# Reordered evacuations and value stages in a one-core kernel of block-sorted attention and four experts

## The chip, the cores and the metric

The program runs on one core of a Trainium2 chip. The core has a matrix engine (TensorE, PE in the profile, with its weight loads as PEld), a vector engine (VectorE, DVE), a scalar engine (ScalarE, ACT), GpSimd (POOL) and SyncE (SP). Each engine works through its own instructions in order. Transfers are issued by SP, by ACT or by POOL and are moved by sixteen DMA engines that all queues share. Matrix products are written to PSUM, a small memory of eight banks, and one of DVE or ACT has to read them out ("evacuate" them) before a bank is used again. The metric is the device time of one execution in microseconds (us).

## The reference

Attention comes first. Its inputs q, k and v have 4 batches, 8 heads, 768 positions and 64 values a head; the positions form 8 blocks of 96. A matrix P of 8 x 8 per batch and head is made almost doubly stochastic by five rounds, and then mixes the blocks of k and v:

```python
for _ in range(5):
    P = np.exp(P - np.max(P, axis=-1, keepdims=True))
    P = P / (np.sum(P, axis=-1, keepdims=True) + 1e-09)
    P = P / (np.sum(P, axis=-2, keepdims=True) + 1e-09)
k_sorted = np.einsum('bhij,bhjcd->bhicd', P, k_b)    # the same for v
attn = softmax(scale * q_b @ k_sorted_b.T)           # within a block of 96
attn_out = attn @ v_sorted_b
```

The result is laid out as x with 3072 tokens of 512 values, and goes through four experts, weighted by the normalized domain probabilities p:

```python
out = 0
for e in range(4):
    out += p[:, e:e+1] * (np.maximum(x @ w1[e], 0) @ w2[e])   # w1: 512 x 1024, w2: 1024 x 512
```

## The kernel before

All matrices are held as 16-bit floats. The tokens are cut into twelve chunks of 256: three chunks (c = 0 to 2) for each of four batches (b = 0 to 3). The first layer of an expert on a chunk is `chunk_first` (L770): two groups of sixteen matmuls of 256 columns (L780), each into a PSUM tile `ps_h`. A matmul reads `xT`, the attention's result with the values along the partitions, in four slices `kc`; slice kc holds the head pair kc and is written by one DMA transpose. DVE evacuates a group by a relu times the expert's weight `pb` (L786) into `Hb`.

The second layer, and in the last stages the first one too, are done in a form of the Strassen-Winograd product: seven products of half-size blocks in place of eight, with sums of the blocks before and after. For the second layer the sums of activations are four DVE operations per expert, `h_sums(e, 1)` to `h_sums(e, 4)` (L750, L752, L754, L756), and for batch 0 the results are added into tiles in `room` (L872 to L896).

The order of the work is written by hand: the instructions are issued to the engines in the order of the program. Attention of the next batch is cut into stages (`st_v`, `st_q`, `st_k`, `st_s`, `st_a`, `st_x`, and loads `st_lv`, `st_lk`, `st_n`), and `PLANS` (L614) says after which step of which chunk each of them is issued: `(2, 7, st_v, 2, 0)` is issued in chunk 2 at slot 7, for batch 2 and head pair 0. Slots 0 to 5 follow the six groups of the first layer of a batch-0 chunk, slots 6 to 12 its second layer's products.

- `st_v(b, pr)` (L357) mixes the blocks of v for two heads: two PE matmuls of 384 columns into a PSUM tile of the pool `psA`, and one ACT copy into the tile `vo` in `arena` (L367). The second one of a group of four heads also issues six SP copies from `vo` to `vs` (L375).
- `st_a` (L438) multiplies the exponentials by `vs` (L449), and DVE normalizes the result into `xsl` (L430, L431). It uses `psA` too. The pool has two tiles, used in turn.
- `st_x` (L457) issues the DMA transpose of `xsl` into a slice of `xT` on SP (L465). `st_q` (L380) issues the transpose of q into `q_ring` on SP (L383), which `st_s` (L409, L414) reads. `load_p` (L211, L213) loads `pb` for a chunk on SP, after the first layer of the chunk before.
- SP works in the order of the program, so each of these transfers waits for the ones issued before it, and for a free one of eight completion semaphores.

The last stages begin at chunk 5 (`G0`), and then take the chunks 6 to 11 two at a time. `last_first` (L1160) runs the first layer as `seven(g, n)` (L1080): for each half expert n, seven products p1 to p7 of four matmuls (L1104) into the banks Z, X and Q. ACT copies Z to X after p1 (L1124), p2 adds to Z, and DVE finishes Z into `Hb` (`finish`, L1110); p6, p7 and p4 add to X, with ACT copies of X between them (L1131, L1139), and DVE finishes X. There are two X and two Z banks, used in turn. p1 to p7 of n and of n-1 are interleaved in the loop at L1182. `last_second` (L1199) is the second layer of 256 of these tokens, with its own sums of activations (L1222).

At the start POOL issues the loads of q, k, v, of expert 0's `w1` (two transfers, L134) and `w2` (one, L139), builds masks between them (L174 to L198), and PE runs matmuls on a constant tile `dummy` to keep warm (`warm`, L252; `keep_warm`, L474).

Of the kernel before, what the change touches and what calls it, by code (L numbers as in the profile page):

```python
# [17 lines left out]
def kernel(  # L18
# [11 lines left out]
    nc = tc.nc  # L30
# [104 lines left out]
                w1sb[e][:, ds(i * n, n)], moe_w1[e].rearrange("(kc p) f -> p kc f", p=P)[:, ds(i * n, n)]  # L135
            )

    def load_w2(e):
        nc.gpsimd.dma_start(w2sb[e][:], moe_w2[e].rearrange("(fc p) d -> p fc d", p=P))  # L139

    def load_half_queries(hf):
        for qd in range(2):
# [1 line left out]
                q0[ds(64 * qd, 64), hf].rearrange("p h r d -> p h (r d)"), half_queries(qd, hf)  # L144
            )

    dummy = Hflat[:, ds(2 * NFC * 2 * P, P)]
    nc.vector.memset(dummy, 0.5)


    NT = N // P
# [1 line left out]
    def p_part(at, n):  # L153
# [12 lines left out]
    load_natural(0, "v", 0)  # L166
    load_natural(0, "k", 1)
    load_natural(0, "v", 1)
    load_w1(0, 2)

    eye16 = const.tile([P, CP], F16, name="eye16")
    maskk = const.tile([P, P], F16, name="maskk")
# [5 lines left out]
        maskk.rearrange("p (i c) -> p i c", c=CP),  # L178
        eye16.rearrange("p (o c) -> p o c", o=1).broadcast_to([P, NB, CP]),
    )  # L180

    perm = const.tile([BLK, BLK], F16, name="perm")
    nc.gpsimd.tensor_copy(
# [90 lines left out]
    scol = const.tile([GH, NB, 1], F32, name="scol")  # L274
    sn16 = const.tile([GH, NB, NB, CP], F16, name="sn16")
    warm(84)
    p_steps = spread_weights()
    nc.gpsimd.tensor_copy(ident6, ident[0:R, 0:R])
    for it in range(5):
        nc.scalar.activation(sn[:], sn[:], AF.Exp, bias=0.0, scale=1.0)  # L280
        if it == 4:
            for qd in range(2):
                h_q(qd, 0, nc.scalar.copy)
            warm(30)
        nc.vector.tensor_reduce(srow[:], sn[:], AX.X, ALU.add)
# [195 lines left out]
    def mix_half(nm, qd, hf, pool, warm_up=0):  # L481

        ps = pool([P, 1024], F32, f"ps_m{nm}_{qd}_{hf}")
        keep_warm(ps[:, 0:P], warm_up)
        tails[(nm, qd, hf)] = ps[:, 2 * R * 64:1024].bitcast(F16).rearrange("p (n x) -> p n x", n=2)
        ps = ps[:, 0:2 * R * 64].rearrange("p (s r x) -> p s r x", s=2, r=R)
        for sg in range(2):
            for r in range(R):
                for hh in range(2):
                    h = 4 * qd + 2 * sg + hh  # L490
                    nc.tensor.matmul(
                        ps[ds(D * hh, D), sg, r, :],
                        head(0, nm, h)[:, r, :],
                        PI0[hf][:, h, :, :].rearrange("p i c -> p (i c)"),
                        start=True, stop=True,
                    )
        return ps
# [111 lines left out]
    def st_bk(b, qd):  # L609
# [10 lines left out]
            (1, 8, st_s, 1, 1), (1, 8, st_x, 1, 0), (1, 9, st_k, 1, 2), (1, 9, st_q, 1, 3), (1, 9, st_lv, 2, 1),  # L620
            (1, 11, st_a, 1, 1), (1, 12, st_lk, 2, 0),
            (2, 0, st_s, 1, 2), (2, 0, st_x, 1, 1), (2, 0, st_n, 2, 0), (2, 0, st_n, 2, 1), (2, 1, st_k, 1, 3),
            (2, 1, st_n, 2, 2), (2, 1, st_n, 2, 3), (2, 2, st_lk, 2, 1), (2, 3, st_a, 1, 2),
            (2, 4, st_x, 1, 2), (2, 4, st_q, 2, 0), (2, 5, st_s, 1, 3),
            (2, 5, st_q, 2, 1), (2, 6, st_a, 1, 3), (2, 7, st_v, 2, 0), (2, 8, st_x, 1, 3), (2, 8, st_v, 2, 1),
            (2, 9, st_k, 2, 0), (2, 9, st_lv, 3, 0), (2, 9, st_n, 3, 0), (2, 11, st_s, 2, 0), (2, 12, st_q, 2, 2),
        ],
        1: [
# [168 lines left out]
    def chunk(b, c, slot, done=()):  # L797
# [68 lines left out]
        if c:  # L866
            both = ob.rearrange("p (h d) -> p h d", h=2)
            times(bankA, blk(0, 0), "b11", es)
            slot()
            times(bankB, blk(1, 0), "b21", es)  # L870
            slot()
            tt(oa1, bankA, oa1, ALU.add)  # L872
            tt(oa1, bankB, oa1, ALU.add)
            h_sums(E - 1, 2)
            times(bankC, blk(1, 1), "n4", es[:1], True, False)
            times(bankQ, sm(0), "t1", es)
            tt(ob2, bankQ, ob2, ALU.add)
            slot()
            for e in es:
                h_sums(e, 3)  # L880
            for e in es:
                h_sums(e, 4)
            times(bankA, sm(1), "t2", es, False)
            tt(oa2, bankA, oa2, ALU.add)
            slot()
            next(sums0)
            times(bankC, blk(1, 1), "n4", es[1:], False)
            tt(ob1, bankC, ob1, ALU.add)
            slot()
            times(bankA, sm(2), "t3", es, False)  # L890
            tt(both, bankA.rearrange("p (o d) -> p o d", o=1).broadcast_to([P, 2, DH]), both, ALU.add)
            slot()
            store(1, ob)
            next(sums0)
            times(bankQ, sm(3), "b22", es, False)
            tt(oa2, bankQ, oa2, ALU.add)  # L896
            slot()
            store(0, oa)
            return
# [180 lines left out]
    def seven(g, n):  # L1080

        lead = g == G0
        if lead:
            e, f0, cols = n, 0, P
            pb = pbs[divmod(g, R // 2)]
            home = lambda i, j: Hb[:, e, ds(i * KH, KH), ds(j * P, P)]
            weight = lambda j: pb[:, ds(e, 1), ds(j * P, P)]
            n -= 1
            Q = last["Q"][(0, 0, 1, 3)[e]][:]
        else:  # L1090
            e, f0, cols = n // 2, n % 2 * 2, 2 * P
            home = lambda i, j: (last["H"][e] if j else Hb[:, e])[:, ds(i * KH + f0, 2), :]
            weight = lambda j: pbs[g](j, e)
            Q = last["Q"][n % 4][:]
        m = 512 // cols
        a, t = As[e], Bs[g]
        X, Z = [last[nm][n % len(last[nm])][:] for nm in ("X", "Z")]
        u2, u3, t22, t12 = [last[nm][n % len(last[nm])] for nm in ("u2", "u3", "t22", "t12")]
        tt = nc.vector.tensor_tensor

        def product(dst, lhs, rhs, first=False):
            for f in range(m):
                for k in range(2):
                    nc.tensor.matmul(  # L1104
                        dst[:, ds(f * cols, cols)], a[lhs][:, k, ds((f0 + f) * P, P)], t[rhs][:, k, :],
                        start=(first and f == 0 and k == 0), stop=(f == m - 1 and k == 1), skip_group_check=True,
                    )

        def finish(i, j, src):
            nc.vector.scalar_tensor_tensor(  # L1110
                out=home(i, j), in0=src.rearrange("p (f x) -> p f x", f=m), scalar=0.0,
                op0=ALU.max, in1=weight(j).broadcast_to([P, m, cols]), op1=ALU.mult,
            )

        def finish2(i, j, src):
            nc.scalar.activation(src, src, AF.Relu, bias=0.0, scale=1.0)  # L1116
            nc.gpsimd.tensor_tensor(  # L1117
                home(i, j), src.rearrange("p (f x) -> p f x", f=m),
                weight(j).broadcast_to([P, m, cols]), ALU.mult,
            )  # L1120

        def p1():
            product(Z, "a11", "b11", True)
            nc.scalar.copy(X, Z)  # L1124
# [12 lines left out]
        def p7():  # L1137
            product(X, "s3", "t3")
            nc.scalar.copy(u3, X)  # L1139
            tt(t22, Q, u3, ALU.add)  # L1140

        def p4():
            product(X, "a22", "t4")
            finish(1, 0, X)

        def p3():
            product(Q, "s4", "b22")
            tt(t12, Q, u2, ALU.add)  # L1148

        return {  # L1150
            1: p1, 2: p2, 3: p3, 4: p4, 5: p5, 6: p6, 7: p7,
            22: lambda: finish2(1, 1, t22), 12: lambda: finish2(0, 1, t12),
        }

# [5 lines left out]
    def last_first(g, slot=None):  # L1160
# [21 lines left out]
        for e in range(1 + lead, N7):  # L1182
# [4 lines left out]
                prs[e - 2][12]()  # L1187
            if not lead or e > 2:
                now[5]()
            now[2]()  # L1190
            now[6]()
            prev[22]()
            prev[4]()
            prev[3]()
        now[7]()
        prev[12]()
# [2 lines left out]
    def last_second(g, now=None, upper=False):  # L1199
# [48 lines left out]
            sums(e, 2)  # L1248
        product(bankC, blk(1, 1), "n4")
        nc.scalar.copy(ob1, bankC)  # L1250
        for e in range(E):
            sums(e, 4, True)
        if lead:
            for e in range(E):
# [8 lines left out]
        if not lead:  # L1263
            for e in range(E):
                sums(e, 3, True)
        early = 1 if final else 2
        for bank, part, _ in ends:
            product(bank[:, part], blk(1, 0), "b22", False, range(early), part=part)
        if closing and not final:
# [27 lines left out]
    ]  # L1297


    mk0 = mix_half("k", 0, 0, psm, 8)  # L1300
    mixed("k", 0, mk0, 0, 2, act)
    mv0 = mix_half("v", 0, 0, psa)
    mixed("v", 0, mv0, 0, 2, vec)
# [2 lines left out]
    mixed("k", 0, mk0, 2, 2, act)  # L1306
    vec(Rs.rearrange("p g (a i) -> p a g i", a=2), Rv.rearrange("p a i g -> p a g i"))
    load_half_queries(1)
    load_w2(0)
    build_PI0(nc.gpsimd, 1, 0, H, Rs[:, 0:H, HB:NB])  # L1310
    h_w(0, vec, 0, 2, tails[("v", 0, 0)])
    mixed("v", 0, mv0, 2, 2, vec)
# [13 lines left out]
    h_s(0, 1, ps_s01)  # L1326
    w01(act)
    ps_a10 = psa([P, 2, 512], F32, "ps_a10")
    keep_warm(ps_a10[:, 0, 0:P], 4)
    h_a(1, 0, ps_a10)  # L1330
    next(p_steps)
    group0(0, 1, 0, [0, 1])
# [138 lines left out]
```

The softmax here doesn't subtract the row's maximum and nothing guards it: scores larger than these inputs give would overflow.

## Time and profile before

| what | value |
| --- | --- |
| median of 4 runs | 364.58 us |
| lowest and highest run | 363.54 and 372.66 us |
| the profiled execution | 364.26 us |
| its span, first to last instruction | 362.5 us |
| mean granted PE clock | 0.998 of full |
| busy: DVE, ACT, POOL | 272.1, 172.6, 133.6 us |
| largest group of matmuls | L780, x576, 67.7 us |
| DMA moved | 40.52 MB |

Busy time is the time in which an engine has at least one instruction running; matmuls overlap, so the distance between their starts says more than their length. In a timeline a line gives the start, the length, the engine, the program's line, the operation, what is written and read, and how many neighbouring instructions the line merges; in brackets stands the idle time of the engine just before, and who ended it. A line of the waits gives an engine and its line, who ended the wait, the microseconds in total, how often, and the longest.

### The profile page before, as it was taken

How to read it: one execution, taken by the hardware profiler on the slowest of the kernel's cores; microseconds unless marked ns; L12 is line 12 of the kernel's file. 1: busy time of each engine (PE TensorE's matmuls, PEld its weight loads, DVE VectorE, ACT ScalarE, POOL GpSimd, SP SyncE). 2: the span in 40 equal slices, each digit the busy share in tenths (PEclk: the TensorE clock that was granted, in tenths of full speed). 3: DMA queues.
4: the chain of work that ended last, by engine and by line, in shares of the span. 5: the costliest groups of instructions: out<-in, count | busy, mean ns of one | idle time of the engine just before them, and what ended most of it. 6: DMA issues, size and time to landing. Idle time of an engine off the chain costs nothing.

```text
span 362.5 us, 9496 instructions
## 1 busy us (share of the span) xinstructions
PE 353.8 (98%) x3949; PEld 306.6 (85%) x3949; DVE 272.1 (75%) x549; ACT 172.6 (48%) x306; POOL 133.6 (37%) x148
## 2 busy tenths in 40 slices
PE   8899999999999899999999999999999999999995
PEld 8785858888888788888889888888888888888895
DVE  5654897779698677768878977895587876678962
ACT  2664330453315255367937258830388611688210
POOL 8882010475022330000526318840068800288300
PEclk9999999999999999999999999999999999999999
DMA  8999999999999999935994410006200014100011
GB/s 110 207 206 230 214 209 198 200 183 192 191 161 135 195 127 151 183 79 72 170 197 81 110 67 0 2 2 124 101 11 2 3 57 118 61 0 2 2 72 46
DMA packets 72007, 40.52 MB, mean 112 GB/s; under 512 B 40598, under 2 KB 66716, under 8 KB 71964
## 3 DMA queue, kind: packets, MB, share of 16 engines
q0 software_dynamic: 36560, 19.93, 41.6%
q1 hardware_dynamic: 35260, 19.92, 28.9%
q8 instruction: 31, 0.51, 0.6%
q14 instruction: 12, 0.10, 0.1%
q10 hardware_dynamic: 144, 0.07, 0.1%
HBM read 42.13 MB, written 6.34 MB: 134 GB/s over the span
## 4 chain that ended last, share of the span: by engine, by line
PE 87%; DMA 5%; DVE 3%; SPq 1%; POOL 1%; ACT 1%; issue 1%; DVEq 0%; ACTq 0%; POOLq 0%
PE ps_Q L1217 17%; PE ps_h L780 16%; PE ps_X L1104 10%; PE ps_p L764 8%; PE ps_Z L1104 7%; PE ps_Q L1104 7%; PE ps_Z L1217 6%; PE ps_h L669 3%; DMA arena<-in_v_dram 3%; PE ps_o L704 3%; PE ps_p L815 3%; DMA vs<-arena 2%; PE ps_a L449 1%; PE ps_s L414 1%; SPq L375 1%; PE ps_v L361 1%
## 5 line engine op out<-in xcount | busy, mean ns | idle before, releaser
L780 PE MATMUL ps_h<-xT,w 128*128 128x256 f16 x576 | 67.7, 273 | 0.0
L780 PEld LDWEIGHTS <-w 128*128 128x128 f16 x576 | 55.2, 98 | 7.3
L786 DVE SCALAR_TENSOR_TENSOR Hb<-ps_h,pb 128x1024 f16<-128x1024 f32 x34 | 41.5, 1224 | 16.9 <-PE ps_h L780 16.8
L1104 PEld LDWEIGHTS <-w 128*128 128x128 f16 x480 | 43.5, 98 | 6.4 <-issue 0.3
L1117 POOL TENSOR_TENSOR arena<-tmp,pb 128x512 f16<-128x512 f32 x12 | 15.3, 1276 | 65.8 <-PE ps_Z L1104 49.9
L1217 PEld LDWEIGHTS <-Hb 128*128 128x128 f16 x320 | 31.2, 98 | 3.6
L1116 ACT ACTIVATE tmp<-tmp 128x512 f32<-128x512 f32 x46 | 29.3, 637 | 3.2 <-DVE tmp L1148 2.6
L1217 PEld LDWEIGHTS <-Sb 128*128 128x128 f16 x304 | 28.2, 98 | 3.0
L1104 PEld LDWEIGHTS <-arena 128*128 128x128 f16 x312 | 27.7, 98 | 2.9
L421 ACT ACTIVATE ET<-ps_s 96x768 f16<-96x768 f32 x24 | 18.1, 802 | 25.4 <-PE ps_s L414 25.2
L404 ACT CAST kT<-ps_k 64x384 f16<-64x384 f32 x48 | 22.8, 474 | 14.1 <-PE ps_k L395 13.1
L121 POOL DMA_DIRECT2D arena<-in_q_dram x24 | 19.9, 840 | 18.9 <-DMA q_ring<-arena 18.7
L1104 PE MATMUL ps_X<-ET,arena 128*128 128x256 f16 x168 | 25.2, 272 | 0.0
L1124 ACT COPY ps_X<-ps_Z 128x512 f32<-128x512 f32 x27 | 15.4, 570 | 19.9 <-PE ps_Z L1104 15.6
L764 PEld LDWEIGHTS <-Hb 128*128 128x128 f16 x232 | 21.9, 98 | 3.0
L1217 PE MATMUL ps_Q<-w,Hb 128*128 128x256 f16 x192 | 24.4, 273 | 0.0
L1104 PE MATMUL ps_Z<-xT,w 128*128 128x256 f16 (+1 forms) x176 | 22.5, 257 | 0.2 <-ACT ps_X L1124 0.2
L1140 DVE TENSOR_TENSOR tmp<-ps_Q,tmp 128x512 f32<-128x512 f32 x20 | 13.8, 692 | 11.3 <-ACT tmp L1139 7.6
L1110 DVE SCALAR_TENSOR_TENSOR Hb<-ps_X,pb 128x512 f16<-128x512 f32 x27 | 18.4, 683 | 1.5 <-PE ps_X L1104 1.5
L1131 ACT COPY tmp<-ps_X 128x512 f32<-128x512 f32 x26 | 15.2, 586 | 9.0 <-PE ps_X L1104 8.6
L750 DVE TENSOR_TENSOR Sb<-Hb 128x512 f16<-128x512 f16 x33 | 19.5, 610 | 0.0
L1110 DVE SCALAR_TENSOR_TENSOR Hb<-ps_Z,pb 128x512 f16<-128x512 f32 x27 | 18.4, 683 | 1.3 <-PE ps_Z L1104 1.3
(261 smaller groups left out, 746.1 us busy)
## 6 DMA issues: line engine op xcount, KB each, us to landing
w<-in_moe_w_dram POOLq DMA_DIRECT2D x7, 1024.0 KB, 27.9
pb<-p_dram SPq DMA_DIRECT2D x9, 512.0 KB, 7.2
arena<-in_k_dram POOLq DMA_DIRECT2D x8, 384.0 KB, 9.7
arena<-in_v_dram POOLq DMA_DIRECT2D x8, 384.0 KB, 8.0
vs<-arena SPq DMA_DIRECT2D x36, 66.0 KB, 5.7
arena<-in_q_dram POOLq DMA_DIRECT2D x24, 96.0 KB, 9.3
out_dram<-ob SPq DMA_DIRECT2D x9, 256.0 KB, 2.1
out_dram<-oa SPq DMA_DIRECT2D x8, 256.0 KB, 2.4
```

What stands on the lines that cost most here:

```text
L121: nc.gpsimd.dma_start(t[:, h // 2, :, h % 2, :], q[b, h].rearrange("(t p) d -> p t d", p=P))
L404: nc.scalar.copy(kT[ds(D * hh, D), r], pk[ds(D * r, D), hh].rearrange("p a (i c) -> p a i c", c=CP),)
L421: nc.scalar.activation(ETs[2 * (pr % 2) + hh][:, 0:S].rearrange("c (a x) -> c a x", a=2), pss[hh][0:BLK, :, 0:HS], AF.Exp, bias=0.0, scale ...
L750: tt(sm[0], blk(0, 1), blk(1, 1), ALU.add)
L764: nc.tensor.matmul(ps, lhs(e, f), Ts[e][rhs][:, f, :], start=(first and e == es[0] and f == 0), stop=(done and e == es[-1] and f == KH - 1 ...
L780: nc.tensor.matmul(ps[:, f, :], w1sb[e][:, kc, ds((4 * g + f) * P, P)], xT[:, kc, ds(2 * c * P, 2 * P)], start=(kc == 0), stop=(kc == NKC ...
L786: nc.vector.scalar_tensor_tensor(out=Hb[:, homes.get(e, e), ds(4 * g, 4), :], in0=ps[:], scalar=0.0, op0=ALU.max, in1=weights(e).broadcast ...
L1104: nc.tensor.matmul(dst[:, ds(f * cols, cols)], a[lhs][:, k, ds((f0 + f) * P, P)], t[rhs][:, k, :], start=(first and f == 0 and k == 0), st ...
L1110: nc.vector.scalar_tensor_tensor(out=home(i, j), in0=src.rearrange("p (f x) -> p f x", f=m), scalar=0.0, op0=ALU.max, in1=weight(j).broadc ...
L1116: nc.scalar.activation(src, src, AF.Relu, bias=0.0, scale=1.0)
L1124: nc.scalar.copy(X, Z)
L1217: nc.tensor.matmul(ps, lhs(e, f), Ts[e][rhs][:, f, part], start=(first and e == 0 and f == 0), stop=(e == E - 1 and f == KH - 1), skip_gro ...
```

## The change

1. In `PLANS[0]` the two stages `st_v(2, 0)` and `st_v(2, 1)` are issued at the slots 2 and 4 of chunk 2 instead of 7 and 8. The second one comes after `st_x(1, 2)` and before `st_q(2, 0)`.
2. In the second and third chunk of batch 0 (`if c:` in `chunk`) the fourth sums are issued after the second product into bank A and its addition, not before.
3. In `last_first`, outside the lead chunk, p2 is split: the product is issued where it was, and finishing Z is issued after p4, so that X of the half expert before is finished first.
4. In `last_second`, outside the lead chunk, only the first one or two experts' fourth sums are issued before the third sums; the others come after them.
5. Expert 0's `w1` is loaded in four quarters (half of the rows, half of the columns), issued after the masks; its `w2` in two halves.
6. The warm-up tile is 512 columns wide: 30, 8 and 4 matmuls of 128 columns become 8, 2 and 1 of 512.

```diff
-    def load_w2(e):
-        nc.gpsimd.dma_start(w2sb[e][:], moe_w2[e].rearrange("(fc p) d -> p fc d", p=P))
+    def load_w2(e, parts=1):
+        n = NFC // parts
+        for i in range(parts):
+            nc.gpsimd.dma_start(
+                w2sb[e][:, ds(i * n, n)], moe_w2[e].rearrange("(fc p) d -> p fc d", p=P)[:, ds(i * n, n)]
+            )
+
+    def load_w1_quarters(e):
+        hk, hf = NKC // 2, FF // 2
+        for i in range(2):
+            for j in range(2):
+                nc.gpsimd.dma_start(
+                    w1sb[e][:, ds(i * hk, hk), ds(j * hf, hf)],
+                    moe_w1[e].rearrange("(kc p) f -> p kc f", p=P)[:, ds(i * hk, hk), ds(j * hf, hf)],
+                )
...
-    dummy = Hflat[:, ds(2 * NFC * 2 * P, P)]
-    nc.vector.memset(dummy, 0.5)
+    broad = Hflat[:, ds(2 * NFC * 2 * P, 4 * P)]
+    dummy = broad[:, 0:P]
+    nc.vector.memset(broad, 0.5)
...
-    load_w1(0, 2)
...
+    load_w1_quarters(0)
...
     warm(84)
+    ps_W = psM.tile([P, 512], F32, tag="ps", name="ps_W")[:]
...
-            warm(30)
+            for m in range(8):
+                nc.tensor.matmul(ps_W, dummy, broad, start=True, stop=True)
...
-            (2, 1, st_n, 2, 2), (2, 1, st_n, 2, 3), (2, 2, st_lk, 2, 1), (2, 3, st_a, 1, 2),
-            (2, 4, st_x, 1, 2), (2, 4, st_q, 2, 0), (2, 5, st_s, 1, 3),
-            (2, 5, st_q, 2, 1), (2, 6, st_a, 1, 3), (2, 7, st_v, 2, 0), (2, 8, st_x, 1, 3), (2, 8, st_v, 2, 1),
+            (2, 1, st_n, 2, 2), (2, 1, st_n, 2, 3), (2, 2, st_lk, 2, 1), (2, 2, st_v, 2, 0), (2, 3, st_a, 1, 2),
+            (2, 4, st_x, 1, 2), (2, 4, st_v, 2, 1), (2, 4, st_q, 2, 0), (2, 5, st_s, 1, 3),
+            (2, 5, st_q, 2, 1), (2, 6, st_a, 1, 3), (2, 8, st_x, 1, 3),
...
             for e in es:
                 h_sums(e, 3)
+            times(bankA, sm(1), "t2", es, False)
+            tt(oa2, bankA, oa2, ALU.add)
             for e in es:
                 h_sums(e, 4)
-            times(bankA, sm(1), "t2", es, False)
-            tt(oa2, bankA, oa2, ALU.add)
...
+        def p2_first():
+            product(Z, "a12", "b21")
+
+        def p2_last():
+            finish(0, 0, Z)
...
-            now[2]()
+            now[2 if lead else 20]()
             now[6]()
             prev[22]()
             prev[4]()
+            if not lead:
+                now[21]()
             prev[3]()
...
-        for e in range(E):
+        early = 1 if final else 2
+        for e in range(E if lead else early):
             sums(e, 4, True)
...
         if not lead:
             for e in range(E):
                 sums(e, 3, True)
-        early = 1 if final else 2
+            for e in range(early, E):
+                sums(e, 4, True)
...
-    mk0 = mix_half("k", 0, 0, psm, 8)
+    mk0 = mix_half("k", 0, 0, psm, 2)
...
-    load_w2(0)
+    load_w2(0, 2)
...
-    keep_warm(ps_a10[:, 0, 0:P], 4)
+    nc.tensor.matmul(ps_a10[:, 0, :], dummy, broad, start=True, stop=True)
```

More of the change, by code (lines that the diff above doesn't have):

```diff
@@ L483, in mix_half @@
         ps = pool([P, 1024], F32, f"ps_m{nm}_{qd}_{hf}")
-        keep_warm(ps[:, 0:P], warm_up)
+        for _ in range(warm_up):
+            nc.tensor.matmul(ps[:, 0:4 * P], dummy, broad, start=True, stop=True)
         tails[(nm, qd, hf)] = ps[:, 2 * R * 64:1024].bitcast(F16).rearrange("p (n x) -> p n x", n=2)
@@ L1150, in seven @@
         return {
-            1: p1, 2: p2, 3: p3, 4: p4, 5: p5, 6: p6, 7: p7,
+            1: p1, 2: p2, 3: p3, 20: p2_first, 21: p2_last, 4: p4, 5: p5, 6: p6, 7: p7,
             22: lambda: finish2(1, 1, t22), 12: lambda: finish2(0, 1, t12),
```

## The prediction

> **What bounds the kernel now.** I read the page first (busy time and the chain), then the waits of TensorE (PE), and then the timeline around each wait, engine by engine. The page says that PE is the bound:
>
> ```profile
> PE 353.8 (98%) x3949; PEld 306.6 (85%) x3949; DVE 272.1 (75%) x549; ACT 172.6 (48%) x306; POOL 133.6 (37%) x148
> ...
> PE 87%; DMA 5%; DVE 3%; SPq 1%; POOL 1%; ACT 1%; issue 1%; DVEq 0%; ACTq 0%; POOLq 0%
> ```
>
> The change removes almost no PE work, so it can only win what PE loses in holes. The waits of PE alone (line, releaser, total, times, longest):
>
> ```profile
> PE ps_a L449 <- DMA vs<-arena: 1.7, 1, 1.7
> ...
> PE ps_p L764 <- DVE room L884: 0.3, 1, 0.3
> ```
>
> These two are the holes that moved lines can reach. The timeline of PE around both, then the DMA queue of SyncE (SP) around the second:
>
> ```profile
> 88.89 1.04 PE L764 MATMUL ps_p<-T,Hb 128*128 128x256 f16 x8
> 90.26 1.47 PE L764 MATMUL ps_p<-T,Sb 128*128 128x256 f16 x12 [0.33 <-DVE room L884]
> ...
> 117.30 1.91 PE L780 MATMUL ps_h<-xT,w 128*128 128x256 f16 x16
> 119.05 0.50 PE L395 MATMUL ps_k<-arena 128*128 128x128 f16 x6
> 119.39 3.66 PE L780 MATMUL ps_h<-xT,w 128*128 128x256 f16 x32
> 124.72 0.64 PE L449 MATMUL ps_a<-vs,ET 96*128 96x65 f16 x16 [1.67 <-DMA vs<-arena]
> ```
>
> ```profile
> 106.07 3.33 SPq L383 DMA_TRANSPOSE q_ring<-arena  x2
> 109.50 0.53 SPq L213 DMA_DIRECT2D pb<-p_dram  x1
> 110.12 1.22 SPq L465 DMA_TRANSPOSE xT<-xsl  x1
> 112.46 4.98 SPq L375 DMA_DIRECT2D vs<-arena  x6
> ```
>
> Sixteen 256-column matmuls start 1.75 us apart (117.30 to 119.05), 0.109 each. So eight from 88.89 are issued by 89.76, and the next waits to 90.26: a hole of 0.50. The 32 from 119.39 are issued by 122.88, and the next waits to 124.72: 1.84, the largest of the kernel. There the six copies of vs leave SP last, after the q_ring transposes, the pb load and the xT transpose.
>
> The third place is the three stages of the last pairs, from about 211, 261 and 310 us. One round of the seven products, put together from the timelines of PE, VectorE (DVE) and ScalarE (ACT):
>
> ```profile
> 226.42 0.60 PE L1104 MATMUL ps_X<-ET,w 128*128 128x256 f16 x4
> 226.72 0.68 DVE L1110 SCALAR_TENSOR_TENSOR Hb<-ps_Z,pb 128x512 f16<-128x512 f32 x1
> 227.31 0.68 DVE L1110 SCALAR_TENSOR_TENSOR Hb<-ps_X,pb 128x512 f16<-128x512 f32 x1
> 228.11 0.57 ACT L1124 COPY ps_X<-ps_Z 128x512 f32<-128x512 f32 x1 [0.29 <-DVE Hb L1110]
> 228.73 0.27 PE L1104 MATMUL ps_Z<-xT,w 128*128 128x256 f16 x1
> ```
>
> The copy into bank X waits until DVE has emptied X, DVE empties Z first, and the second product into Z waits for the copy. A round is 28 matmuls, 3.06 us. The first products into Z start at 214.86, 217.92, 221.02, 224.12, 227.29 and 230.47: 3.06, 3.10, 3.10, 3.17, 3.18. Together 0.31 over the ideal, and 0.12 more after the last one: 0.43 us lost per stage.
>
> **The sum, part by part.** It is made against the profiled execution: 364.26 us, span 362.5 and 1.76 around it; the median of the four runs is 364.58.
>
> *Order of finishing Z and X.* Two DVE operations change places, none is added. PE's product into X starts at 226.42; elsewhere (235.43, operation at 236.07) DVE follows such a start by 0.64, so emptying X can begin at 227.06 instead of 227.31 and ends about 0.25 sooner. DVE then stands still for some 0.3 that it now works; its four operations of 0.60 fill 2.4 of 3.06, and the sum for t12, now behind, ends about 0.3 later. Its reader on ACT (L1116) comes about where it ends and is followed by 0.17 of idle time. The copy then waits for PE as it did in the first round (215.55, no hole). Bounds 0 (t12 or ACT becomes late) and 0.43 x 3 = 1.3; I take -1.3, since the first round already runs so.
>
> *Sums in order of use.* L884 takes 0.42 behind three L756 (1.0). In front of them it ends near 89.2, before 89.76. The third sums are done; the fourth ones end near 90.1 and their product starts at 91.5. So -0.50 in the chunk at 90 us. In the next chunk the same edit meets a hole of 0.19 (113.95 to 114.14), which the next part swallows.
>
> *Sums in the last stages.* No hole stands before those products (236 to 260 us), and DVE, working between 250.97 and 257.2 with the same operations, is at least 1.4 early for each reader. 0; if a reader were late, at most one sum, 0.34, per stage.
>
> *Two value stages sooner.* Each moves two matmuls (0.33 of PE), one ACT copy (0.80) and, from the second one, six vs copies on SP; the v load that overwrites the same rows (POOL, 111.90) is freed some 7 us sooner too. The old hole goes: vs would leave SP by about 111 and had 7 to 8 us to landing, the reader comes at 123: -1.84. But SP issues in order, and vs now stands before both q_ring transposes, the pb load and the xT transpose for the last head pair of batch 1. That xT is read by the fourth matmul of the group at 117.30, at 117.63. No view prints its landing; the trace's sixteen completion marks for it run from 117.35 to 117.50. It has 0.13 us to spare.
>
> Working SP forward: the xT transpose before it leaves at 105.0 to 106.2 (104.69 plus 0.33 for the first moved stage). Six vs issues took 4.98 here and 4.09 at 81.18: to 110.3 or 111.2; with 0.62 each to 109.9. Two q_ring issues take 2.4 to 3.3. So pb leaves between 112.4 and 114.5; I take 112.8, 3.3 later. pb landed 7.2 after its issue here, 5.2 where nothing else ran (202.7), 8.3 at 138.6, and xT landed 0.8 behind it. So xT lands at 120.8 (118.4 to 123.6): a new hole of +3.2 (0.8 to 6.0) at the fourth matmul. I take the transfer's own row, 7.2, because the same transfers stand before it. This hole also swallows the small terms before it: the wait of the second moved stage for its PSUM buffer (DVE frees it near 104.2, PE arrives at 103.8: 0.4), less the 0.19 and 0.1 that go. The q_ring transpose lands at about 114.7 (4.6 after issue) for a reader at 115.6.
>
> *Expert 0's matrices in parts.* The w1 issues now follow the mask operations, four instead of two at 0.72: POOL reaches its half of sn16 at 11.4 instead of 11.11; the reader at 14.06 needs it by then and gets it at 13.0. The second half of w2 waits for the last v load (15.76), so POOL's build of PI0 starts near 16.7 instead of 14.95; its reader comes at 22.8. In exchange parts land sooner: w1's halves landed at 18.3 and 20.8, 2.5 apart, in the order of issue, so quarters come at about 17.0, 18.3, 19.6, 20.8. The group that reads the first began at 18.52, but waited for the ACT copy L502 (17.99 to 18.47), so nothing is won. w2 landed at 27.9, where its reader began; halves save about 0.1. Bounds -0.2 and +0.3 (smaller pieces); -0.1.
>
> For that splitting the Trainium skill has a rule against it: "DMA: Bandwidth & Descriptors", section "Anatomy of one DMA", gives each DMA from POOL a fixed 2.0 us, and its rules for authors ask for one MiB and more. If pieces paid that one after another, three more would make an estimated 6 us, and the sum would be 369.7. Here a queued half came 2.5 after the other, and 1024 KB of w2 4.8 after the load before it, so the queue shows no such price.
>
> *Wider warm-ups.* 30 narrow matmuls (1.85) become 8 of 512 columns, at 0.24 each (L704, 0.97 for four) 1.9; PE then waits 0.79 for DVE anyway. 8 become 2 and 4 become 1, within 0.05; the first ends before DVE frees PI0. The larger memset starts PE up to 0.2 later, inside the same wait. 0, between -0.1 and +0.2.
>
> Sum: -1.3 - 0.50 - 1.84 + 3.2 - 0.1 = -0.5, so 364.26 - 0.5 = **363.7**.
>
> **Rivals.** *The new hole stays small* (xT by 118.5, hole under 1.0). For: pb alone took 5.2, and POOL's queue was empty between 106 and 116. Against: two transposes stand right before it. Sum -3.7 + 0.8 = -2.9: 361.3. *The new hole outgrows all gains* (slower). Place: the same fourth matmul; break-even at a hole of 3.7, xT at 121.4; slower by 0.5% from 123.2. For: transposes behind pb took 10.2 (issued 86.4) and 11.6 (139.3), which would put xT at 123.6 to 125. Against: POOL loads of 384 KB ran there. Price +2.2 at 123.6: 366.5. *The finishing order wins nothing*, because t12 and ACT's reader become late: -0.5 + 1.3 = +0.8: 365.0.
>
> **How the numbers follow.** Forecast (hole 1.5 to 4, seven products won) 0.50, 362.0 to 364.6; small hole 0.25; large hole 0.15; no gain in the seven 0.10. The 80% range drops the outer parts of the small and the large hole: 361.0 to 366.0. A measurement here tells about 0.5%, 1.8 us, from no change. Faster by more (under 362.4): the small hole and a tenth of the forecast, 0.29. Slower by more (over 366.1): two thirds of the large hole and a little, 0.11. The rest, 0.60.
>
> **What would show it.** Right: no wait of PE on vs; the transposes of q_ring, the pb load and xT about 3 us later on SP; a wait of PE on xT for 2 to 4 us at the first group of batch 1; L884 ahead of L756 and no hole at 90; rounds of 3.06 in the last stages; starts of the first layer unmoved. Wrong: PE not waiting on xT (then 361), a wait on q_ring or pb instead, rounds still at 3.17, or the first layer waiting for w1 or w2.

## The result and the profile after

The changed kernel takes 365.77 us, the median of 38 executions, beside 364.25 us for the kernel before: a ratio of 1.0033, with a 95% interval of 1.0021 to 1.0046. The ratios in this document are estimated from the fast executions alone, so they are not the quotient of the two medians (here 1.0042). The forecast was 363.7; the kernel is slower by 1.2 us by the ratio, and by 1.5 by the medians, where 0.5 less was forecast. The profiled execution took 365.64 us (before: 364.26), its span is 363.8 (362.5). The two lines of the page that answer to those of before:

```profile
PE 353.4 (97%) x3918; PEld 305.3 (84%) x3918; DVE 274.8 (76%) x549; ACT 172.8 (47%) x306; POOL 135.1 (37%) x151
...
PE 90%; DVE 4%; DMA 2%; ACT 1%; issue 1%; DVEq 0%; ACTq 0%
```

PE still sets the time. Its waits alone, in the changed kernel (engine and line, who ended the wait, total, times, longest):

```profile
PE ps_h L798 <- DMA xT<-xsl: 2.8, 1, 2.8
PE ps_w L271 <- DVE Hb L162: 1.5, 1, 1.5
PE ps_R L329 <- DVE sn L317: 1.0, 1, 1.0
PE ps_mk L509 <- ACT kT L520: 0.7, 1, 0.7
PE ps_v L378 <- DVE xsl L448: 0.3, 1, 0.3
```

The wait on `vs` is gone, and so is the one for VectorE at 90 us. A wait of 2.8 us on `xT` stands at the place the prediction named. New beside it are 0.7 us in the first layer (`ps_mk`) and 0.3 at the second moved value stage (`ps_v`). SP's queue and PE's timeline around the large one:

```profile
105.00 1.21 SPq L482 DMA_TRANSPOSE xT<-xsl  x1
106.30 3.79 SPq L392 DMA_DIRECT2D vs<-arena  x6
110.20 3.42 SPq L400 DMA_TRANSPOSE q_ring<-arena  x2
113.72 0.54 SPq L228 DMA_DIRECT2D pb<-p_dram  x1
114.36 1.23 SPq L482 DMA_TRANSPOSE xT<-xsl  x1
```

```profile
117.53 0.49 PE L798 MATMUL ps_h<-xT,w 128*128 128x256 f16 x3
120.86 2.38 PE L798 MATMUL ps_h<-xT,w 128*128 128x256 f16 x13 [2.83 <-DMA xT<-xsl]
123.03 0.85 PE L412 MATMUL ps_k<-arena 128*128 128x128 f16 x6
123.67 4.25 PE L798 MATMUL ps_h<-xT,w 128*128 128x256 f16 x32
127.76 0.41 PE L466 MATMUL ps_a<-vs,ET 96*128 96x65 f16 x8
```

The six `vs` copies now stand ahead of `q_ring`, `pb` and `xT`, and the last `xT` transpose leaves SP at 114.36 instead of 110.12. By the trace's completion marks it landed at 120.81, and the fourth matmul starts at 120.86. What follows is just as telling: thirteen matmuls of 256 columns take 2.17 us (120.86 to 123.03), 0.167 each instead of 0.109, and the next 32 take 4.09 instead of 3.49. The clock is the reason. The same execution cut into stretches (stretch, its length, PE busy and instructions, granted clock, DMA share, GB/s):

```profile
110.00:118.00 8.00, 8.00 (x88) 1.00 1.04 160
118.00:121.00 3.00, 0.17 (x3) 1.00 1.24 182
121.00:125.00 4.00, 4.00 (x26) 0.57 1.21 223
125.00:130.00 5.00, 5.00 (x59) 1.00 1.32 123
```

A mean of 0.57 over 4.0 us is full clock for some 0.6 and half clock for 3.4; the trace's own record of the clock has half from 121.47 to 124.89. By the starts above, the three groups behind the wait took 0.75, 0.30 and 0.60 longer than at full clock: 1.65 us.

This does not happen in every execution. Of the 38, twelve show a mean granted clock of 0.999 or 1.0 and have a median of 364.2 us, the same as before; 26 show 0.989 to 0.995 and have 366.0. The mean does not tell where in an execution the clock fell; but in the three kernels below that begin alike and have no long wait (the value stages back, the copies behind `xT`, the wait filled), none of 24 executions, all on one chip, shows less than 0.998. Of 105 executions of the kernel before that were run beside the kernels below, five show a clock under 0.997.

Where the profiled time went, read from starts of the same matmul in both traces:

| mark on PE | before | after | moved |
| --- | --- | --- | --- |
| scores at the end of the first layer | 36.54 | 37.01 | +0.47 |
| scores behind the hole at 90 us | 95.20 | 95.18 | -0.02 |
| fourth matmul of the group that reads `xT` | 117.63 | 120.86 | +3.23 |
| first matmul that reads `vs` | 124.72 | 127.76 | +3.04 |
| ahead of the last stages | 174.33 | 177.46 | +3.13 |
| last wait for ACT, behind them | 355.44 | 357.25 | +1.81 |
| span | 362.5 | 363.8 | +1.3 |

Between the last two marks 0.5 comes back because the last store landed 1.7 after its issue, not 2.2. Between 177 and 357 us the seven products gain 1.32, as forecast.

### The profile page after: what moved, and what is told of

The parts are those of the page before. It is cut to its first block, busy times and chain, and to the rows that moved or that the text cites. A ratio compares the mean times of both kernels' runs of the same rounds, so it can differ in the third digit from the quotient of the medians.

```text
span 363.8 us, 9438 instructions
## 1 busy us (share of the span) xinstructions
PE 353.4 (97%) x3918; PEld 305.3 (84%) x3918; DVE 274.8 (76%) x549; ACT 172.8 (47%) x306; POOL 135.1 (37%) x151
## 4 chain that ended last, share of the span: by engine, by line
PE 90%; DVE 4%; DMA 2%; ACT 1%; issue 1%; DVEq 0%; ACTq 0%
PE ps_h L798 17%; PE ps_Q L1243 17%; PE ps_p L782 10%; PE ps_X L1122 10%; PE ps_Z L1122 7%; PE ps_Q L1122 6%; PE ps_Z L1243 6%; PE ps_h L687 3%; PE ps_o L722 3%; PE ps_p L833 3%; DMA xT<-xsl 2%; PE ps_s L431 1%; PE ps_a L466 1%; PE ps_v L378 1%; PE ps_k L412 1%
## 5 line engine op out<-in xcount | busy, mean ns | idle before, releaser
L798 PE MATMUL ps_h<-xT,w 128*128 128x256 f16 x576 | 69.6, 276 | 2.8 <-DMA xT<-xsl 2.8
L768 DVE TENSOR_TENSOR Sb<-Hb 128x512 f16<-128x512 f16 x33 | 20.3, 633 | 0.0
L1172 DVE TENSOR_TENSOR tmp<-ps_Q,tmp 128x512 f32<-128x512 f32 x26 | 17.7, 682 | 0.8 <-PE ps_Q L1122 0.8
```

Of the source, the lines that this page charges most:

```text
L768: tt(sm[0], blk(0, 1), blk(1, 1), ALU.add)
L798: nc.tensor.matmul(ps[:, f, :], w1sb[e][:, kc, ds((4 * g + f) * P, P)], xT[:, kc, ds(2 * c * P, 2 * P)], start=(kc == 0), stop=(kc == NKC ...
```

## Theories and experiments

**Theory:** the loss sits in the moved value stages alone. The six copies make `xT` late, PE waits 3 us, and behind an idle stretch of that length the clock is granted at half. **Rivals:** the first layer (0.47 late) or the sums are the loss; the clock falls for a reason other than idleness; doing the value stages sooner costs by itself. The line numbers below are those of each kernel.

**The value stages back.** The changed kernel with one edit:

```diff
-            (2, 2, st_v, 2, 0), ... (2, 4, st_v, 2, 1), (2, 4, st_q, 2, 0),
+            ... (2, 7, st_v, 2, 0), (2, 8, st_x, 1, 3), (2, 8, st_v, 2, 1),
```

> The changed kernel with the two value stages put back into their old slots, all else as changed. Theory (the loss sits in the new wait on xT at 117.9 to 120.9 us and in the half clock behind it, 121.5 to 124.8 us): no wait of PE on xT, the old wait on vs of about 1.8 us is back near 124 us, the mean granted clock is 0.998 or more in every execution. Sum: 364.3 - 1.3 (seven products) - 0.5 (sums at 90 us) + 0.5 (first layer, 0.47 late at 37 us) = 363.0, a ratio of 0.9965. Rival (the loss sits in the first layer or in the sums): 365 or more, because both are still in.

Measured: 361.38 us, ratio 0.9937 (0.9916 to 0.9958), clock 0.999 or 1.0 in all six executions. PE around the place:

```profile
117.68 1.91 PE L798 MATMUL ps_h<-xT,w 128*128 128x256 f16 x16
119.43 0.50 PE L412 MATMUL ps_k<-arena 128*128 128x128 f16 x6
119.76 3.66 PE L798 MATMUL ps_h<-xT,w 128*128 128x256 f16 x32
123.26 0.65 PE L466 MATMUL ps_a<-vs,ET 96*128 96x65 f16 x16
```

The loss goes with the two stages: 365.8 becomes 361.4, with the first layer and the sums still in. The rival of the first layer falls. But 361.4 is 1.6 below my 363.0, because the old wait on `vs` did not come back: no idle time stands before the reader at 123.26. That part of the theory was wrong, and later experiments are about it. The two kernels were timed beside different executions of the kernel before; by their ratios, 1.0033 and 0.9937, the two stages cost 3.5 us, by the medians 4.4.

**The value stages alone.** The kernel before with only those lines of `PLANS` changed.

> The kernel before with the two value stages moved and nothing else. Theory: the SP queue issues the last xT transpose of batch 1 about 3.4 us later, PE waits some 3 us for it, the old wait on vs (1.84) goes, and in most executions the clock is granted at half for 3.4 us behind the wait, which costs 1.65. Sum: 364.3 + 3.4 - 1.8 = 365.9 with the clock kept, 367.5 with the clock halved, the median near 367 (ratio 1.007), executions in two groups by clock. Rival (as the prediction's step had it: the wait costs its length alone): 365.7 and a clock of 0.998 throughout. Rival (the first layer is the loss): 364.3 or less.

Measured: 367.59 us, ratio 1.0106 (1.0071 to 1.0142). Four executions show a clock of 0.990 to 0.995 and 367.5 to 370.6 us, two show 0.998 or more and 365.8 and 366.3. The profiled one is of the two:

```profile
118.34 0.49 PE L780 MATMUL ps_h<-xT,w 128*128 128x256 f16 x3
121.90 1.58 PE L780 MATMUL ps_h<-xT,w 128*128 128x256 f16 x13 [3.07 <-DMA xT<-xsl]
123.32 0.50 PE L395 MATMUL ps_k<-arena 128*128 128x128 f16 x6
```

Here the same thirteen matmuls take 1.42 us behind a wait of 3.07, at full clock. So the wait and the half clock are two things, and the second one is a matter of chance at this length.

What the chance is about can be read from the traces' records of the clock. Every stretch at full clock that ends inside a trace is a whole multiple of 3.413 us long (116.05 in the changed kernel and 354.99 in the kernel before are 34 and 104 of them), and where in the span these windows begin differs from one execution to another. In the changed kernel the window from 118.06 to 121.47 holds 2.80 of the 2.83 us that PE stands idle, and the next window is the one at half clock. Here a boundary at 120.30 parts the idle 3.07 us into 1.46 and 1.60, and no half clock follows. Two traces fit this reading, and a third one below; that the boundary decides in every execution is not shown.

**The copies behind `xT`.** The changed kernel, with PE and ACT doing the value stages sooner as in the change, but the six copies issued after the transpose:

```diff
-        if pr % 2:
+        if pr % 2 and (b, pr) != (2, 1):
+            st_vs(b, pr)
...
-            (2, 6, st_a, 1, 3), (2, 8, st_x, 1, 3),
+            (2, 6, st_a, 1, 3), (2, 8, st_x, 1, 3), (2, 8, st_vs, 2, 1),
```

> The changed kernel, but the six vs copies of the second moved value stage are issued only behind the last xT transpose of batch 1, so that SP issues in the old order; PE and ACT still do the two value stages sooner. Theory (what is dear is only the place of the six copies on SP): xT lands at about 117.5 again, PE waits for it less than 0.5; vs leaves SP by 116 and lands by 121 to 123.5, against 124.6 before, for a reader at about 122.9, so a wait of 0 to 0.8 on vs. Sum: 363.0 (as with the stages back) - 1.84 + 0.4 = 361.6, between 361.1 and 362.5, ratio about 0.993, clock 0.998 or more. Rival (doing the value stages sooner costs by itself, by PSUM waits or by the v load freed sooner): 363 or more.

Measured: 361.44 us, ratio 0.9938 (0.9921 to 0.9956), clock 0.998 or more in all executions. Neither `xT` nor `vs` is waited for; PE's idle 0.3 at the moved stage stays:

```profile
110.54 1.62 SPq L486 DMA_TRANSPOSE xT<-xsl  x1
112.25 5.00 SPq L396 DMA_DIRECT2D vs<-arena  x6
```

So it is only the place of the six copies on SP that is dear. Doing the work sooner is not; it wins nothing either, against the stages in their old slots.

**The wait filled.** The changed kernel, with repeats of the first matmul put in front of the group that waits for `xT` (they write what the group then writes again):

```diff
+                    if (b, c, e, g, f) == (1, 0, es[0], 0, 0):
+                        for _ in range(20):
+                            nc.tensor.matmul(
+                                ps[:, f, :], w1sb[e][:, 0, ds(4 * g * P, P)], xT[:, 0, ds(2 * c * P, 2 * P)],
+                                start=True, stop=True,
+                            )
```

> The changed kernel with 20 repeats of the first matmul of the first group of batch 1 in front of it (20 x 0.109 = 2.2 us); they are overwritten by the group itself, and nothing else is changed. The wait on xT ends when it did, at about 120.9 us, but PE stands idle for only about 0.8 of it. Theory (the half clock follows from PE standing idle for most of 3.4 us): no stretch at half clock behind the wait, mean granted clock 0.998 or more in every execution, 364.1 (ratio 0.9995), as the executions of the changed kernel have it that show a clock of 0.999. Rival (the clock falls for another reason, or the wait costs what it does whatever the clock): 365.8, a clock of 0.995 in two thirds of the executions.

Measured: 364.14 us, ratio 1.0008 (0.9996 to 1.0021), clock 0.998 or more in all twelve executions.

```profile
117.55 2.35 PE L799 MATMUL ps_h<-xT,w 128*128 128x256 f16 x20
119.74 0.49 PE L804 MATMUL ps_h<-xT,w 128*128 128x256 f16 x3
121.06 1.58 PE L804 MATMUL ps_h<-xT,w 128*128 128x256 f16 x13 [0.83 <-DMA xT<-xsl]
122.48 0.50 PE L412 MATMUL ps_k<-arena 128*128 128x128 f16 x6
```

`xT` comes no sooner (121.06), and PE does 2.2 us of useless work. Yet the median is 1.6 below that of the changed kernel, because the thirteen matmuls behind the wait run at full clock. The half clock follows from PE standing idle.

**Filled by less.** The same with 5 repeats in place of 20, which leaves 2.24 us idle.

> The changed kernel with only 5 repeats in front of the first group of batch 1 (0.55 us), so that PE stands idle for about 2.3 us of the wait on xT instead of 2.83 (0.83 with 20 repeats). Theory (the clock is judged over stretches of 3.4 us that start without regard to the program, and falls when PE stands still for more than some 2.0 of one): between the two, the clock falls in about half of the executions, 364.1 in those with a clock of 0.998 or more and 365.8 in the others. Rival (the length of the wait decides, not the idle time): two thirds fall, as in the changed kernel. Rival (only idle times near 3 us count): none falls, 364.1.

Measured: 364.07 us, ratio 1.0007 (0.9983 to 1.0032). Three of twelve executions show 0.994 or 0.995 and 365.7 to 367.0; nine show 0.999 or 1.0 and 363.2 to 364.3. A quarter is less than the half that I expected, and speaks against two thirds. It does not refute "none": of 23 executions of the kernel before in the same set, without this wait, three also show a clock under 0.997, and the mean does not tell where it fell. The profiled execution kept full clock; there a boundary of the windows, at 119.90, parts the idle 2.24 us into 1.33 and 0.91.

**The seven products alone**, in the kernel before (`now[2 if lead else 20]()` and `now[21]()` of the change and nothing else).

> The kernel before with only the seven products' finishing order changed. Up to about 211 us its instructions are those of before. Theory: the rounds of the three last stages are 3.06 each, no hole before the second product into Z, 1.3 less: 363.0, ratio 0.9965. Rival (the finishing order wins nothing): 364.3. Besides, it is a second look at the old wait on vs near 124 us, which was 1.84 in the profile of before and is 0 with the stages put back: if it is again near 1.8, one of the other parts took it away; if it is small or absent, it differs from one execution to another.

Measured: 363.49 us, ratio 0.9993 (0.9966 to 1.0021). The interval includes 1 and ends just short of the expected 0.9965, so the time alone does not show the gain; the medians lie 1.0 apart (364.45 for the kernel before). The trace tells more: all rounds of the three stages are 3.05 or 3.06 apart. In this execution some loads of the first layer landed late, which put it 0.76 behind at 37 us and 0.5 behind ahead of the last stages; it gains 1.3 in them. The wait on `vs` is there:

```profile
PE ps_a L449 <- DMA vs<-arena: 1.4, 1, 1.4
```

**The sums alone**, in the kernel before.

> The kernel before with only the order of the sums changed (chunks of the first batch and last stages). Theory: the hole of 0.50 at 90 us goes, in the last stages nothing moves, 0.5 less: 363.8, ratio 0.9986, with the wait on vs near 124 us as before. If the wait on vs also goes in this kernel, the order of the sums is what took it away when the stages were put back, and the time is near 362.

Measured: 364.13 us, ratio 1.0005 (0.9971 to 1.0038), not told apart from no change. In the trace the hole at 90 us is gone: the mark at 95.20 gains 0.48 on the mark at 86.79. The wait on `vs` stands at 1.8 (the profile names no releaser here; the last copy landed at 124.99 and its reader starts at 125.08). As expected, nothing moved in the last stages.

**The loads in parts alone**, in the kernel before.

> The kernel before with only expert 0's matrices loaded in parts. Theory: the second k product of the first batch is given another PSUM buffer (the one whose copy ACT ends at 15.34, not the one that VectorE frees at 14.78), so it starts at 15.38 instead of 14.84 and PE is 0.5 late from there to 37 us: 364.7, ratio 1.001. Rival (the prediction's -0.1): the start at 14.84, 36.4 at the mark that before has at 36.54. Besides: if the wait on vs near 124 us is gone with the later start, the time is near 363.

Measured: 364.77 us, ratio 1.0013 (0.998 to 1.0046). The second k product is late, by the same wait for ACT as in the changed kernel:

```profile
14.63 0.42 PE L532 MATMUL ps_mv<-ident,Sb 128*96 128x128 f16 x4
15.77 0.57 PE L505 MATMUL ps_mk<-Sb,arena 128*64 128x64 f16 x24 [0.71 <-ACT kT L516]
```

The profiled execution also ran its first layer at half clock from about 16.7 to 20.2 us, so its own time can't be used for the rest.

**The wide warm-ups alone**, in the kernel before; first one execution, then twelve.

> The kernel before with only the wider warm-up matmuls. Theory: the PSUM buffers stay as before, the second k product starts at 14.84 and the mark at 36.54 stays within 0.1; 364.3. Rival (the wide warm-ups make the first layer late): the mark near 37.0, as in the changed kernel.

Measured: 365.51 us in one execution, which also ran at half clock near 17 to 21 us and landed two loads late. The second k product has its old PSUM buffer and waits for a load instead, so it says nothing for or against the warm-ups. The twelve:

> The kernel before with only the wider warm-up matmuls again, now timed. Theory W (the wide warm-ups are what cuts the old wait on vs near 124 us): no wait there, the first layer as before in most executions: 364.2 - 1.8 = 362.4, ratio 0.995. Rival (the wait was absent in the first look only because PE came there 2.3 late after a half clock in the first layer): 364.2, ratio 1.0, with a wait of 1.6 to 2.0 wherever the first layer is on time. The prediction's step for this part was 0, between -0.1 and +0.2.

Measured: 363.02 us, ratio 0.9971 (0.9957 to 0.9985). The first layer is on time (36.53), and before the reader of `vs` 0.15 us of idle time is left. The gain sits at that wait: the reader starts at 123.17 instead of 124.72. The warm-ups that I had costed at 0 gain 1.0.

**w1 in halves again**, with the value stages in their old slots, and the same with the copies behind `xT`:

```diff
+    load_w1(0, 2)
...
-    load_w1_quarters(0)
```

> The changed kernel with the two value stages in their old slots and with w1 of expert 0 loaded in two halves at its old place again (w2 in halves, wide warm-ups, the sums and the seven products stay). Theory on the first layer (the quarters of w1 moved the second k product into the PSUM buffer of the first one): it starts at 14.84 instead of 15.4 and the mark at 37.01 to 37.3 us comes back to 36.5; 361.4 - 0.5 = 360.9, ratio 0.9915. Rival (the late start is a late landing of the loads, whatever the buffer): the mark stays near 37.0 and the time at 361.4. Besides, on the old wait on vs (gone with the stages back, 1.6 to 2.0 with the seven products or the sums alone): if it returns here, the quarters of w1 had removed it, and the time is 362.5.

Measured: 361.53 us, ratio 0.9939 (0.9917 to 0.996). The second k product waits for VectorE again, and the mark is at 36.44:

```profile
14.19 0.42 PE L535 MATMUL ps_mv<-ident,Sb 128*96 128x128 f16 x4
14.77 0.57 PE L508 MATMUL ps_mk<-Sb,arena 128*64 128x64 f16 x24 [0.16 <-DVE Rs L1334]
```

In the changed kernel the same product reads:

```profile
14.24 0.42 PE L536 MATMUL ps_mv<-ident,Sb 128*96 128x128 f16 x4
15.38 0.57 PE L509 MATMUL ps_mk<-Sb,arena 128*64 128x64 f16 x24 [0.72 <-ACT kT L520]
```

Who ends the wait tells which PSUM buffer the product waits for. With the quarters (the changed kernel, the loads alone) it is ACT's copy of the first k product into `kT`, without them (the kernel before, this one) VectorE's read of `ps_R` into `Rs`, though w2 is still in halves here. So the quarters of w1 moved the second k product into another buffer; by what order the buffers are given out no run shows. The 0.5 won at the start is not in the time (361.53 us, and 361.38 with the quarters): small waits on `xT` (0.18) and `vs` (0.23) stand later in this execution.

> The kernel with the vs copies issued behind the last xT transpose, and with w1 of expert 0 in two halves at its old place again. Theory: the mark at 36.5 again; the vs copies wait for nothing but SP, so they leave before 116 whatever the start does, and PE waits for neither xT nor vs: 361.4 - 0.5 = 360.9, ratio 0.9915, clock 0.998 or more. Rival (the vs copies are late again as in the kernel before): a wait of up to 1.8 on vs near 123 us, up to 362.7.

Measured: 361.88 us, ratio 0.9936 (0.9913 to 0.9959), with no wait on `xT` or `vs` and the mark at 36.71. The first layer is on time here too, and the gain of 0.5 does not show in the median of seven executions.

**What takes the old wait on `vs` away?** First the kernel before with the seven products, the sums and the wide warm-ups, that is, the change without its value stages and loads:

> The kernel before with the seven products, the sums and the wide warm-ups changed, but expert 0's matrices loaded as before and the value stages in their old slots: what is left of the change when both of its dear parts are out. Theory A (the old wait on vs near 124 us is cut by the loads in parts, since it was 1.6 to 2.0 without them): the wait is near 1.8 again, 364.3 - 1.3 - 0.5 = 362.5, ratio 0.995. Theory B (it is cut by the earlier sums and is not tied to the loads): a wait under 0.5, 361.0 to 361.5, ratio 0.992.

Measured: 360.74 us, ratio 0.9919 (0.9894 to 0.9944), the best of all kernels here. Neither `xT` nor `vs` is waited for:

```profile
116.75 1.91 PE L784 MATMUL ps_h<-xT,w 128*128 128x256 f16 x16
118.49 0.50 PE L398 MATMUL ps_k<-arena 128*128 128x128 f16 x6
118.83 3.66 PE L784 MATMUL ps_h<-xT,w 128*128 128x256 f16 x32
122.32 0.65 PE L452 MATMUL ps_a<-vs,ET 96*128 96x65 f16 x16
```

So the loads are not needed for it. Next the same with narrow warm-ups, and the same with wide ones but as many PE instructions as before (`warm(119)` and 4 wide matmuls in place of 84 and 8):

> The kernel before with the seven products and the sums changed and the narrow warm-ups kept. Theory W (the wide warm-ups cut the wait on vs): the wait is 1.6 to 2.0 again, 364.2 - 1.3 - 0.5 = 362.4, ratio 0.995. Rival (the sums together with an early first layer cut it): a wait under 0.5 and 360.7, as with the wide warm-ups.

Measured: 362.58 us, ratio 0.9963 (0.9938 to 0.9988), executions from 361.2 to 366.0, and a wait of 0.52 in the profiled one: between the two expectations.

> The seven products, the sums and the wide warm-ups as in the kernel without the loads in parts, but with 35 narrow warm-up matmuls more and 4 wide ones fewer, so that PE executes as many instructions in all as in the kernel before; the warm-up as a whole is 1.1 longer, inside the wait for VectorE that follows it. Theory C (what matters is where the kernel's 16 KB blocks of PE instructions end, so when they are fetched): the wait on vs is back, 1.6 to 2.0, and the time 362.4. Rival (the count does not matter, the wide warm-ups act by their own work): no wait, 360.7.

Measured: 362.44 us, ratio 0.9965 (0.9939 to 0.9992), executions from 361.1 to 366.2 and one of 369.4, and a wait of 0.55: again between the two. Its longer warm-up also made the first layer 0.6 late. This experiment told nothing apart.

What the profiles with the stages in their old slots show together: the last of the six copies landed 7.8, 8.0, 8.5, 7.0 and 6.7 us after its issue in the five with narrow warm-ups (before, seven products, sums, loads in parts, seven products with sums). It landed 6.7 and 5.2 us after it with the wide warm-ups alone (the timed and the first execution), 5.2, 6.9 and 5.9 in three more with wide ones (without the loads, w1 in halves, stages back), and 6.7 with `warm(119)` and four wide ones. The two groups meet at 6.7 to 7.0. The wait is what this transfer leaves over. Why it is shorter stays open; that the warm-ups shorten it is a difference of two small groups of executions and of one timed ratio, and no mechanism was shown.

## Why the prediction was wrong

The step that failed is *Two value stages sooner*: it priced the new hole by its length alone.

- *"a new hole of +3.2 at the fourth matmul"*. Place and cause were right, and the order on SP was the one worked out. That `xT` was put at 120.8 and landed at 120.81 is partly luck: `pb` left SP at 113.72, not 112.8, and landed 6.24 after its issue, not 7.2, and the two misses cancel. What was left out is what a hole of this size does to the clock. It cost 1.65 more in the profiled execution and 1.8 between the two groups of executions (366.0 and 364.2), in 26 of 38. No rival named the clock. With that term the sum of 363.7 becomes 365.4.
- *"The old hole goes: -1.84"*. It goes as worked out: the last copy landed at 114.34 in the changed kernel, and at 114.01 with the stages alone. But it is not the stages' own gain: with them in their old slots, the other parts of the change take the wait away too, wholly or mostly, which the prediction did not see. So in this change the two stages are worth not 3.2 - 1.84 = +1.4 but, against the kernel with the stages back, 365.8 - 361.4 = +4.4 by the medians: 2.8 of it with the clock kept, the rest by the clock.

The Trainium skill has the rule that was needed, in "TensorE: Matmul & The Clock Gate". "What's actually happening" says that the clock is judged over windows of 3413 ns that run on without regard to the kernel, and "Why this matters for your kernels" asks for no idle gaps over about 3 us. The traces agree: the half clock here lasted 3.41 us, and the full stretches are whole multiples of 3.413. On the size of the gap the runs go further: behind 2.83 us of idle time the clock fell in most of 38 executions (26 show a low mean), and behind 0.83 in none of 12; for 2.24 us the 3 of 12 do not decide.

The other steps:

- *Order of finishing Z and X, -1.3*: right by the traces. PE's products into Z and VectorE's order in the changed kernel:

```profile
224.12 0.60 PE L1122 MATMUL ps_Z<-xT,w 128*128 128x256 f16 x4
226.94 0.69 DVE L1128 SCALAR_TENSOR_TENSOR Hb<-ps_X,pb 128x512 f16<-128x512 f32 x1 [0.27 <-PE ps_X L1122]
227.17 0.60 PE L1122 MATMUL ps_Z<-xT,w 128*128 128x256 f16 x4
227.54 0.68 DVE L1128 SCALAR_TENSOR_TENSOR Hb<-ps_Z,pb 128x512 f16<-128x512 f32 x1
227.85 0.57 ACT L1142 COPY ps_X<-ps_Z 128x512 f32<-128x512 f32 x1 [0.16 <-PE ps_Z L1122]
230.23 0.60 PE L1122 MATMUL ps_Z<-xT,w 128*128 128x256 f16 x4
```

  The copy waits for PE, no longer for VectorE, and the rounds are 3.05 and 3.06. Measured -1.32.
- *Sums in order of use, -0.50*: right. L900, which was L884, now stands ahead of the fourth sums, and PE's next product follows the one before without idle time. Measured -0.49:

```profile
89.24 0.42 DVE L900 TENSOR_TENSOR room<-ps_p,room 128x256 f32<-128x256 f32 x1
89.58 1.09 DVE L774 TENSOR_TENSOR Sb<-Hb,Sb 128x512 f16<-128x512 f16 x3
90.23 1.47 PE L782 MATMUL ps_p<-T,Sb 128*128 128x256 f16 x12
```

- *Sums in the last stages, 0*: right.
- *Expert 0's matrices in parts, -0.1*: wrong in the first layer, +0.5 at its end, outside the bounds of -0.2 to +0.3; in the whole time no run shows it apart from the noise. The loads themselves were waited for by no one. The cost came through a PSUM buffer that this edit moved, a path on which the step had no row. The pieces landed later than worked out, too: the last quarter at 22.19, not 20.8.
- *Wider warm-ups, 0*: wrong in the average. Alone they gain 1.0 (0.9971), and the bound was -0.1; in the first layer, where the step had its rows, they moved nothing.
- *The rivals.* The slower one, *The new hole outgrows all gains*, came near with its 366.5, but by a hole of 3.7 and more that did not occur. *The finishing order wins nothing* is refuted by the rounds of 3.06.

In the profiled execution the terms that were missed are +1.65 (clock) and +0.57 (first layer, against -0.1), with -0.5 from the last store: together 1.7 of the 1.9 between the forecast of -0.5 and the measured +1.4.

## What to carry to other kernels

When a stage that issues transfers is moved up, list what it overtakes on that queue and find the transfer with the least time to spare; here six copies of 0.63 each on SP made a transpose with 0.13 to spare 3 us late, and issuing the copies behind it cured that without giving up the earlier work. Price an idle stretch of PE of nearly 3 us twice, once by its length and once by the half clock that may follow it, and read the granted clock of every execution before a spread of times is called noise. Read off the built program, not off the source, whether an edit leaves the buffers of later tiles where they were.

## What the runs showed that I had not expected

- Useless matmuls in a wait can pay: 2.2 us of them in front of a wait that they do not shorten took the median from 365.8 to 364.1.
- The half clock also came in the first layer, where PE waits for masks and loads in pieces of 0.2 to 1.1 us: in the profiled execution of the kernel with the loads in parts the clock in the stretches from 14 us on was

```profile
14.00:16.00 2.00, 1.13 (x31) 1.00 1.27 204
16.00:18.00 2.00, 2.00 (x63) 0.68 1.27 214
18.00:20.00 2.00, 2.00 (x25) 0.50 1.22 196
```

  It came in some executions only, and it is a part of the spread of several kernels here. Why in these and not in others is not shown.
- One and the same transfer, six copies of 66 KB each, landed 5.2 to 8.5 us after its last issue from one kernel and execution to another, always with the stages in their old slots, so a wait of 1.84 read from one profile was not a stable amount to be won.
